# Second expert layer of an FFT-and-two-experts kernel: the last column block takes the seven-product form, block ends and quarter sums move

## The chip, the core and the metric

The kernel runs on one core of a Trainium2 chip. Its time is the device time of one execution in microseconds. The version before has a median of 963.82 us over 3 runs (963.35 to 965.81).

## The reference, cut to what matters

```python
def _attn_ref(x):                                  # x: (2, 3008, 256)
    X = np.fft.fft(x, axis=1)
    X = np.fft.fft(X, axis=2)
    return X.real
...
h = x @ w_in                                       # layer 1: (6016, 256) @ (256, 2048)
g = np.maximum(h, 0.0) + alpha * np.minimum(h, 0.0)
y = g @ w_out                                      # (2048, 256)
...
h = x @ w_in                                       # layer 2, same sizes, own weights
g = h * (1.0 / (1.0 + np.exp(-h)))
return (g @ w_out).astype(np.float32)
```

All values are fp32. The kernel splits each operand of a product into a rounded high part and a low rest, and forms a product as three matmuls: high by high, low by high, high by low.

## The kernel before

**Blocks and steps.** The 6016 tokens are handled, by a symmetry of the transform, as 6 column blocks c = 0 to 5 of 512 columns (448 in block 0 of layer 2), each for a sum and a difference half. Layer 1 takes 16 steps per block, 96 in all. Layer 2 takes 8 pairs p per block, 7 steps each; its steps are numbered on from 96 (block 0 is steps 96 to 151, block 1 begins at 152). Work beside the matmuls is tied to step numbers by tables (`T0`, `T1`, `PRE`, `WHEN`, `SUMS`), inside a manual schedule: every engine runs its instructions in the order in which the code issues them.

**Layer 2, one pair.** A 2x2 block product with seven instead of eight half-size products gives h: `trio` issues the seven as M1 to M7, three matmuls each (L875). VectorE and ScalarE add them to the four quarters c11, c12, c21, c22 (`ring`), and ScalarE applies SiLU. Then follows the product with `w_out2`. In blocks 0 and 5 this is `second2`: all eight quarter products, 24 matmuls a pair (L959); each quarter is split by a ScalarE copy (the high part, L894) and a VectorE or GpSimd subtraction (the low part, L899). In blocks 1 to 4 (`FAST`) the output product has the seven-product form as well: four differences T1 to T4 of the quarters (L1072), seven splits (h.. on ScalarE L1073, l.. on VectorE or GpSimd L1085), and seven groups O1 to O7 of three matmuls, 21 a pair (`group`, L1060), accumulated over the eight pairs in PSUM (O2 goes through a bank of its own and is added up by VectorE as E).

**Order in a fast pair.** `SEQ`, `SEQ0`, `SEQ1` and `SEQ2` are token lists, one token for one instruction or one group of three matmuls; "h21-1" is the high part of quarter 21 of the pair before. So the output product of a pair runs among the products of the next one. `SEQ1` (p = 1) also holds the end of the block before: two copies out of PSUM on ScalarE (m5c, m7c), and the adds U2, U3, U4, D12, D21 on VectorE and D22 on GpSimd (`ending`, L1110, L1129).

**Quarter sums and factors.** Each block's layer-1 result x2 is written out and also turned into four quarter sums in place, four GpSimd subtractions of 128x512 (`x2_sums`, L778), which begin three steps after the block's result is saved. Blocks 2 to 5 read these back in layer 2 (`load_raw32`) and split them, one factor a pair, by ScalarE (fh) and GpSimd (fl, L1019). Block 0's and 1's seven factors are made from x2 directly (`factors`, L827, L828, L832).

**Weights of layer 2.** They arrive as 64-bit integers' halves. `narrow` makes floats of them: two ScalarE instructions, a VectorE shift (L241) and an integer add (L243, on GpSimd in the first 16 steps, else on VectorE). Most converted weights are set aside in DRAM (`keep_back`, at the steps `PRE`) and fetched again later; `mixed_wout` and `store_s` (L285 to L298) form sums of the output weights on GpSimd. In layer 1 GpSimd also makes the low part of every activation (gl, L727).

Of the kernel before, what the change touches and what calls it, by code (L numbers as in the profile page):

```python
# [1532 lines left out]
```

## Time and profile before

| | before |
|---|---|
| median of 3 runs | 963.82 us |
| profiled execution, its own time | 967.2 us |
| span in the profile, first to last instruction | 965.3 us |
| mean granted TensorE clock | 0.991 |
| TensorE matmul busy | 939.8 us (97%) |
| VectorE busy | 754.3 us (78%) |
| ScalarE busy | 670.7 us (69%) |
| GpSimd busy | 534.9 us (55%) |

In the profile PE is TensorE, DVE is VectorE, ACT is ScalarE, POOL is GpSimd and SP the engine that issues most transfers. Matmuls overlap in it, so the busy time of PE counts more than what it could not do without; the distance between the starts of matmuls is the better measure.

### The profile page before, as it was taken

To read this page: it belongs to the slowest core of one execution; us is meant where nothing else is said; L and a number is where in the kernel's file an instruction comes from. 1 tells how busy PE (TensorE), PEld (TensorE's weight loads), DVE (VectorE), ACT (ScalarE), POOL (GpSimd) and SP (SyncE) were. 2 spreads that over 40 slices of the span, in tenths; PEclk is the share of its full clock that TensorE was granted. 3 is DMA by queue.
4 is the path that set the end of the run, shared out by engine and by line. 5 is a ranking of instruction groups with operands and counts; after the bars stand their busy time and mean duration, and the time that the engine had idled before them with its cause. 6 is when DMAs were issued, how large, how long until landed. Compare 5 with 4: busy or idle time off the path is not lost.

```text
span 965.3 us, 12665 instructions
## 1 busy us (share of the span) xinstructions
PE 939.8 (97%) x4261; PEld 773.2 (80%) x4261; DVE 754.3 (78%) x1113; ACT 670.7 (69%) x1168; POOL 534.9 (55%) x371
## 2 busy tenths in 40 slices
PE   9999999999999979999989999999999999998998
PEld 9899888888788868888879778768777777776886
DVE  4877665777787797866655689999999999988554
ACT  6887566665665656766655688878878888884554
POOL 0598777677688689999985522323332233232322
PEclk9999999999999999999999999999999999998999
DMA  9311123234616321012221034533344344440001
GB/s 342 138 44 50 50 58 75 55 94 135 216 57 238 109 102 66 29 39 77 66 87 34 31 119 152 173 119 125 134 158 145 117 142 142 154 142 33 12 1 43
DMA packets 50268, 98.99 MB, mean 103 GB/s; under 512 B 6326, under 2 KB 13596, under 8 KB 49180
## 3 DMA queue, kind: packets, MB, share of 16 engines
q1 hardware_dynamic: 49628, 97.36, 30.7%
q8 instruction: 33, 0.54, 0.2%
q10 hardware_dynamic: 576, 0.84, 0.2%
q14 instruction: 31, 0.25, 0.1%
HBM read 64.74 MB, written 33.44 MB: 102 GB/s over the span
## 4 chain that ended last, share of the span: by engine, by line
PE 84%; DVE 8%; issue 4%; ACT 1%; POOL 1%; DMA 1%; DVEq 0%; POOLq 0%; ACTq 0%
PE pso L742 25%; PE psh L875 19%; PE psh L651 13%; PE psm L1060 11%; PE pso L959 7%; PE psB L466 2%; DVE ring L1072 2%; PE psE L1060 2%; PE psU L1283 2%; PE psW L602 1%; DVE ghl L1085 1%; DVE ring L1071 1%; DVE ring L908 1%; DMA ur<-tmid 1%; DVE forms L1085 1%
## 5 line engine op out<-in xcount | busy, mean ns | idle before, releaser
L727 POOL TENSOR_TENSOR gl<-r,gh 128x1024 fp32r<-128x1024 f32 (+1 forms) x96 | 228.0, 2377 | 62.9 <-ACT gh L726 44.7
L875 PE MATMUL psh<-ts,wi 128*128 128x512 f32 (+1 forms) x864 | 238.1, 393 | 5.6 <-DVE ring L1071 3.0
L875 PEld LDWEIGHTS psh<-ts,wi 128*128 128x128 f32 x864 | 160.5, 189 | 48.0 <-DVE ring L1071 10.5
L742 PE MATMUL pso<-gh,wo_o 128*128 128x512 f32 (+1 forms) x768 | 192.8, 388 | 0.0
L742 PEld LDWEIGHTS pso<-gh,wo_o 128*128 128x128 f32 x768 | 145.1, 189 | 27.9
L651 PE MATMUL psh<-pq,wa 128*128 128x512 f32 (+1 forms) x576 | 149.5, 393 | 7.0 <-DVE h L671 7.0
L700 DVE SCALAR_TENSOR_TENSOR psd<-h,psh 128x512 f32<-128x512 f32 (+1 forms) x96 | 65.7, 684 | 98.9 <-PE psh L651 98.5
L651 PEld LDWEIGHTS psh<-pq,wa 128*128 128x128 f32 x576 | 107.5, 189 | 29.4 <-DVE h L671 8.9
L726 ACT ACTIVATE gh<-r 128x1024 fp32r<-128x1024 f32 (+1 forms) x96 | 99.9, 1041 | 36.2 <-DVE r L711 36.0
L1085 DVE TENSOR_TENSOR ghl<-ring,ghl 128x512 fp32r<-128x512 f32 x160 | 117.0, 754 | 0.4
L908 DVE TENSOR_TENSOR ring<-ring,psh 128x448 f32<-128x448 f32 (+1 forms) x112 | 71.3, 652 | 55.5 <-PE psh L875 53.4
L701 ACT ACTIVATE r<-psh 128x512 f32<-128x512 f32 (+1 forms) x96 | 56.6, 589 | 81.6 <-DVE psd L700 74.4
L1073 ACT ACTIVATE ghl<-ring 128x512 fp32r<-128x512 f32 x160 | 96.1, 625 | 10.9 <-DVE ring L1072 10.2
L742 PE MATMUL pso<-gl,wo_o 128*128 128x512 f32 (+1 forms) x384 | 101.4, 385 | 0.0
L1072 DVE TENSOR_TENSOR ring<-ring 128x512 f32<-128x512 f32 x128 | 92.5, 722 | 8.6 <-POOL forms L1085 3.5
L1019 POOL TENSOR_TENSOR ts<-sides,ts 128x512 fp32r<-128x512 f32 x21 | 34.7, 1651 | 109.1 <-ACT ts L1014 109.1
L959 PE MATMUL pso<-ghl,wAo 128*128 128x448 f32 (+1 forms) x324 | 86.1, 381 | 3.5 <-POOL ghl L899 3.5
L742 PEld LDWEIGHTS pso<-gl,wo_o 128*128 128x128 f32 x384 | 72.2, 188 | 13.5
L1085 POOL TENSOR_TENSOR forms<-ring,forms 128x512 fp32r<-128x512 f32 x32 | 41.7, 1302 | 72.5 <-ACT forms L1073 72.5
L1060 PE MATMUL psm<-ghl,sring 128*128 128x512 f32 x288 | 81.3, 396 | 0.0
L911 ACT ACTIVATE ring<-ring 128x448 f32<-128x448 f32 (+1 forms) x64 | 38.6, 602 | 59.8 <-DVE ring L908 59.2
L1073 ACT ACTIVATE ring<-psh 128x512 f32<-128x512 f32 x96 | 56.9, 592 | 33.4 <-PE psh L875 33.4
(145 smaller groups left out, 1616.7 us busy)
## 6 DMA issues: line engine op xcount, KB each, us to landing
sring<-sdr SPq DMA_DIRECT2D x32, 512.0 KB, 4.0
raw<-in_w_in SPq DMA_DIRECT2D x16, 512.0 KB, 5.6
raw<-in_w_out SPq DMA_DIRECT2D x16, 512.0 KB, 5.7
xf<-x SPq DMA_DIRECT2D x8, 1024.0 KB, 4.9
sides<-xf SPq DMA_DIRECT2D x28, 256.0 KB, 4.4
ts<-fdr SPq DMA_DIRECT2D x26, 256.0 KB, 3.6
fdr<-ts SPq DMA_DIRECT2D x24, 256.0 KB, 4.5
out_dram<-ob SPq DMA_DIRECT2D x19, 256.0 KB, 2.7
```

What stands on the lines that cost most here:

```text
L651: T.matmul(bank[:, :w], wa[q][:, mm, eo, a, :], pq[c][:, 2 * eo + bb, :w], start=eo == 0 and a == bb, stop=bb == 1, skip_group_check=True)
L700: V.scalar_tensor_tensor(other[:, :w], t[:, :w], 2.0, bank[:, :w], op0=ALU.mult, op1=ALU.subtract)
L726: A.activation(hi[:, :, :w], r[:, :, :w], AF.Copy)
L727: G.tensor_tensor(lo[:, :, :w], r[:, :, :w], f32(hi[:, :, :w]), op=ALU.subtract)
L742: T.matmul(po[c][s][k][:, :w], wo1[q][:, mm, a, k * P:(k + 1) * P], g[:, s, :w], start=m == 0 and a == 0 and g is hi, stop=m == NF - 1 and ...
L875: T.matmul(dst[:, :w], wi2[p][:, FORMS[j], a], t[:, :w], start=start and a == 0 and t is hi, stop=t is lo, skip_group_check=True)
L908: V.tensor_tensor(dst[:, :w], a[:, :w], bank[j][:, :w], op=ALU.add)
L959: T.matmul(po[c, 2][s][k][:, :w], wo2[q][:, mm + m, a, k * P:(k + 1) * P], outs[p, i][:, g, :w], start=p == 0 and i < 2 and a == 0 and g == 0,
L1060: T.matmul(dst, w, form[f][:, g], start=first and b == g == 0, stop=last and g == 1, skip_group_check=True)
L1072: sub = lambda dst, a, b: V.tensor_tensor(dst, a, b, op=ALU.subtract)
L1073: copy = lambda dst, src: A.activation(dst, src, AF.Copy)
L1085: (G if name in ON_G else V).tensor_tensor(form[f][:, 1], side_of[f], f32(form[f][:, 0]), op=ALU.subtract)
```

## The change

- `FAST` becomes 1 to 5: the last block takes the seven-product output form. Its last pair gets token lists of its own (`K5`, `L5`), and a list `Z` ends the kernel in place of `second2`'s last matmuls and `store`.
- Tokens are given per pair of a block (A, B, C, D, F, N, N, L for blocks 2 to 5; F0, F1, F2, N.. for block 1). A letter g at a token puts it on GpSimd; without it a low part or an add is VectorE's. A token that an earlier list already performed is skipped, so lists can run ahead.
- Block end: five accumulators are copied out by ScalarE (m1c, m3c, m4c, m5c, m7c); only U2 and E add out of PSUM on VectorE; five adds between SBUF tiles (a1 to a5) lie in the third to fifth pair of the next block on GpSimd (in `Z` on VectorE).
- Quarter sums: block 2's at steps 69, 72, 75, 78; block 3's at 103 to 108; block 5's at 126 to 139; block 4's result is read back from DRAM at step 111 (`again`) and summed at 115 to 124.
- `PRE` and `T1` get other steps, and one entry of `STAGE_B` is a step earlier. Block 0's end is stored by single tokens of F0.

```diff
-    FAST = 1, 2, 3, 4
+    FAST = 1, 2, 3, 4, 5
...
+    def again(c, steps):
+        t = spot("px2", [2, 2, CK * N2], F32, "x2")
+        nc.sync.dma_start(flat2(t), flat2(xf[c][0]))
+        SUMS[c] = steps
+        return x2_sums(c, t)
...
-        for _ in range(SUMS):
-            yield EARLY
-        for dst, a, b in ((b11, b12, b11), (b12, b22, b12), (b22, b22, b11), (b21, b21, b22)):
+        for i, (dst, a, b) in zip(SUMS[c], ((b11, b12, b11), (b12, b22, b12), (b22, b22, b11), (b21, b21, b22))):
+            while now[0] < i:
+                yield EARLY
             yield AMID
             SUB.tensor_tensor(dst, a, b, op=ALU.subtract)
...
+    def ending(c, name, other):
+
+        o, u, rest4 = outbuf(c), tail["u"], t1
+        add = lambda dst, a, b: (G if other else V).tensor_tensor(dst, a, b, op=ALU.add)
+        copies = {"m1c": (u, "O1"), "m3c": (o[:, 1, 0], "O3"), "m4c": (rest4, "O4"), "m5c": (o[:, 1, 1], "O5"),
+                  "m7c": (o[:, 0, 1], "O7")}
+        if name in copies:
+            dst, src = copies[name]
+            A.activation(dst, accum[c, src], AF.Copy)
+            copied.add((c, src))
         elif name == "U2":
-            add(u, u, accum[c, "O6"])
-        elif name == "U4":
-            add(o[:, 1, 0], u, o[:, 1, 1])
-        elif name == "D12":
-            add(o[:, 1, 0], o[:, 1, 0], accum[c, "O3"])
+            V.tensor_tensor(u, u, accum[c, "O6"], op=ALU.add)
+        elif name == "a1":
+            add(o[:, 1, 0], o[:, 1, 0], u)
+        elif name == "a2":
+            add(o[:, 1, 0], o[:, 1, 0], o[:, 1, 1])
             write(c, 1, 0)
...
-    ON_G = ('l11', 'fl', 'D22')
...
+        "N": ("h22-1 c12-1 l11-1g M1 E-2 s12-1 h21-1 m1 l22-1 T1-1 T3-1 hT1-1 fh M2 c11 O1-1 M6 u2 s11 O3-1 "
+              "lT1-1 hT3-1 O5-1 T2-1 hT2-1 M7 u3 l21-1 M5 lT3-1 T4-1 O7-1 lT2-1 c22 hT4-1 M4 fl O6-1 h11 "
+              "s21 s22 M3 lT4-1 O2-1 O4-1 "),
...
+        "L5": ("M1 m1 hT1-1 T3-1 l21-1 M2 c11 M6 O1-1 hT3-1 u2 T2-1 M7 T4-1 s11 lT1-1 h11 u3 M5 M4 l11 c22 "
+               "M3 hT2-1 lT3-1 hT4-1 lT2-1 s21 s22 O2-1 c12 O3-1 h21 O1 O6-1 O5-1 O7-1 lT4-1g s12 h22 E-1 "
+               "m1c l21 T1 hT1 l22 T3 O4-1 hT3 O2 T2 T4 O3 lT1 hT2 hT4 lT2 O6 lT3 "),
+        "Z": ("E-1 O7-1 O5-1 U2-1 m3c-1 m7c-1 lT4-1g a1-1 O4-1 m5c-1 a3-1 a2-1 m4c-1 a4-1 a5-1 "),
...
-    SUMS = 3
-    T1 = 42, 44, 48, 49, 50, 51, 52, 54, 54, 56, 58
+    SUMS = {2: (69, 72, 75, 78), 3: (103, 105, 106, 108), 5: (126, 132, 134, 139)}
+    AGAIN = 111, 4, (115, 118, 120, 124)
+    T1 = 40, 42, 46, 47, 48, 49, 50, 51, 53, 54, 55
```

Line numbers in the rows of the changed kernel are its own: 883 is `trio`, 1071 `group`, 1083 and 1084 the adds and subtractions of a pair, 1125 the copies of a block end, 1128 U2, 1120 the adds a1 to a5, 785 the quarter sums, 904 a low part in block 0.

On TensorE, at the end of the program (last pair of block 5; psh are products of `trio`, pso the output banks), 27 matmuls of `second2` stand behind the last product before, of which these are the last 19:

```order
L959 MATMUL pso_7782<-forms,wAo_4799 128x512
L959 MATMUL pso_7780<-ghl,wAo_4799 128x512 x2
L959 MATMUL pso_7782<-ghl,wAo_4799 128x512 x2
L959 MATMUL pso_7780<-ghl,wAo_4799 128x512
L959 MATMUL pso_7782<-ghl,wAo_4799 128x512
L959 MATMUL pso_7783<-forms,wAo_4799 128x512 x2
L959 MATMUL pso_7781<-forms,wAo_4799 128x512 x2
L959 MATMUL pso_7783<-forms,wAo_4799 128x512
L959 MATMUL pso_7781<-forms,wAo_4799 128x512
L959 MATMUL pso_7783<-ghl,wAo_4799 128x512 x3
L959 MATMUL pso_7781<-ghl,wAo_4799 128x512 x3
```

and now, from the last product on (psm and psE are the banks of `group`):

```order
L883 MATMUL psh_8256<-ts,wi_7_4661 128x512 x3
L1071 MATMUL psE<-ghl,wAo_4797 128x512 x3
L1071 MATMUL psm<-forms,sring 128x512 x3
L1071 MATMUL psm<-forms,wAo_4797 128x512 x3
L1071 MATMUL psm<-ghl,sring 128x512 x9
L1071 MATMUL psm<-ghl,wAo_4797 128x512 x6
L1071 MATMUL psm<-forms,sring 128x512 x3
L1071 MATMUL psm<-ghl,sring 128x512 x9
L1071 MATMUL psm<-ghl,wAo_4797 128x512 x3
```

The 27 have become 39: six groups of the pair before and the seven of the last pair itself.

On VectorE, in the second pair of block 3 (the end of block 2 lies there; ob is the output buffer, sides holds u and the running sum E), there stands before:

```order
L1071 TENSOR_TENSOR ring<-ring,psh_6387 128x512
L1071 TENSOR_TENSOR ob<-sides,psm 128x512
L1110 TENSOR_TENSOR sides<-sides,psm 128x512
L1110 TENSOR_TENSOR ob<-ob,sides 128x512
L1072 TENSOR_TENSOR ring<-ring 128x512
L1110 TENSOR_TENSOR ob<-sides,ob 128x512
L1085 TENSOR_TENSOR ghl<-ring,ghl 128x512
L1110 TENSOR_TENSOR ob<-ob,psm 128x512
L1071 TENSOR_TENSOR ring<-ring,psh_6466 128x512
L1072 TENSOR_TENSOR ring<-ring 128x512
L1085 TENSOR_TENSOR forms<-ring,forms 128x512
```

and now:

```order
L1083 TENSOR_TENSOR ring<-ring,psh_6474 128x512
L1128 TENSOR_TENSOR sides<-sides,psm 128x512
L1084 TENSOR_TENSOR ghl<-ring,ghl 128x512 x2
L1084 TENSOR_TENSOR ring<-ring 128x512
L1083 TENSOR_TENSOR ring<-ring,psh_6474 128x512
L1084 TENSOR_TENSOR ghl<-ring,ghl 128x512 x2
L1083 TENSOR_TENSOR ring<-ring,psh_6474 128x512
L1084 TENSOR_TENSOR forms<-ring,forms 128x512
```

Of the adds of the block end (four of the five before are shown, U2, U3, U4 and D12) U2 (L1128) is left; in the place of the others stand instructions of the pair itself.

On GpSimd, in layer 1 around step 70 (gl is the low part of an activation, x the layer-1 result of block 3 before and of block 2 now, stage_s sums of output weights, wi a layer-2 weight tile, pq one row of block 5's input), there stands before:

```order
L727 TENSOR_TENSOR gl<-r,gh 128x1024
L557 TENSOR_TENSOR pq_3120<-pb,pq_3120 1x512
L727 TENSOR_TENSOR gl<-r,gh 128x1024
L778 TENSOR_TENSOR x_3251<-x_3251 128x512
L298 TENSOR_TENSOR stage_s<-stage_s 128x4x128 x2
L727 TENSOR_TENSOR gl<-r,gh 128x1024
L778 TENSOR_TENSOR x_3251<-x_3251 128x512
L727 TENSOR_TENSOR gl<-r,gh 128x1024
L370 TENSOR_TENSOR wi_0_3262<-y_3341,wi_0_3262 128x4x128
```

and now, up to the same weight tile:

```order
L727 TENSOR_TENSOR gl<-r,gh 128x1024 x2
L298 TENSOR_TENSOR stage_s<-stage_s 128x4x128
L727 TENSOR_TENSOR gl<-r,gh 128x1024
L557 TENSOR_TENSOR pq_3113<-pb,pq_3113 1x512
L727 TENSOR_TENSOR gl<-r,gh 128x1024
L785 TENSOR_TENSOR x_2582<-x_2582 128x512
L727 TENSOR_TENSOR gl<-r,gh 128x1024
L370 TENSOR_TENSOR wi_0_3261<-y_3305,wi_0_3261 128x4x128
```

The two sums at this place are one, and the two L298 are further ahead, with a gl between them.

On GpSimd, in block 0 (steps 104 to 112: ghl a low part, wAo an output weight's low part), there stands before:

```order
L382 TENSOR_TENSOR wi_5_4425<-t_98,wi_5_4425 128x4x128
L778 TENSOR_TENSOR x_4448<-x_4448 128x512 x2
L899 TENSOR_TENSOR ghl<-ring,ghl 128x448
L778 TENSOR_TENSOR x_4448<-x_4448 128x512 x2
L324 TENSOR_TENSOR wAo_4176<-y_4506,wAo_4176 128x2x256
L324 TENSOR_TENSOR wAo_4538<-y_4508,wAo_4538 128x2x256
L899 TENSOR_TENSOR ghl<-ring,ghl 128x448
```

and now:

```order
L785 TENSOR_TENSOR x_3249<-x_3249 128x512
L382 TENSOR_TENSOR wi_5_4415<-t_98,wi_5_4415 128x4x128
L785 TENSOR_TENSOR x_3249<-x_3249 128x512 x2
L904 TENSOR_TENSOR ghl<-ring,ghl 128x448
L785 TENSOR_TENSOR x_3249<-x_3249 128x512
L324 TENSOR_TENSOR wAo_4166<-y_4498,wAo_4166 128x2x256
L324 TENSOR_TENSOR wAo_4528<-y_4500,wAo_4528 128x2x256
L904 TENSOR_TENSOR ghl<-ring,ghl 128x448
```

It is block 3's sums that stand here now, four as before, three of them ahead of the first low part.

## Rows read from the trace of the kernel before

**Rows 1.** The page: span, and TensorE's busy time and share of it.

```profile
span 965.3 us, 12665 instructions
PE 939.8 (97%) x4261; PEld 773.2 (80%) x4261; DVE 754.3 (78%) x1113; ACT 670.7 (69%) x1168; POOL 534.9 (55%) x371
```

**Rows 2.** Windows: block 0, 1, 2; block 5's first seven pairs; last pair.

```profile
core 0: us, PE busy (x) PEld busy (x) DVE busy (x) ACT busy (x) POOL busy (x), PEclk, DMA share, GB/s
463.30:543.20 79.90, 76.39 (x361) 68.77 (x360) 49.37 (x74) 48.90 (x90) 60.59 (x57) 0.98 0.18 58
543.20:625.30 82.10, 79.82 (x342) 62.37 (x341) 73.00 (x108) 66.47 (x121) 24.60 (x18) 1.00 0.39 129
625.30:705.70 80.40, 79.64 (x338) 61.73 (x337) 77.60 (x118) 67.42 (x123) 23.66 (x17) 1.00 0.43 141
...
866.70:945.80 79.10, 74.94 (x312) 60.71 (x313) 50.85 (x77) 42.22 (x71) 20.87 (x15) 0.96 0.04 14
945.80:965.30 19.50, 15.83 (x70) 12.76 (x68) 9.04 (x14) 8.21 (x14) 4.70 (x3) 1.00 0.14 54
```

**Rows 3.** Timeline of the end: start us, us, engine, instructions, [idle before <-releaser].

```profile
958.75 1.52 PE L959 MATMUL pso<-forms,wAo 128*128 128x512 f32 x6
...
960.11 1.52 PE L959 MATMUL pso<-ghl,wAo 128*128 128x512 f32 x6
...
961.67 0.60 ACT L972 ACTIVATE ob<-pso 128x512 f32<-128x512 f32 x1 [2.35 <-PE pso L959]
962.29 0.35 ACTq L976 DMA_DIRECT2D out_dram<-ob  x1
```

**Rows 4.** Timelines of VectorE and GpSimd in a steady pair of block 3.

```profile
764.26 1.19 DVE L1085 TENSOR_TENSOR ghl<-ring,ghl 128x512 fp32r<-128x512 f32 x1
...
767.65 2.13 DVE L1072 TENSOR_TENSOR ring<-ring 128x512 f32<-128x512 f32 x3
769.70 0.68 DVE L1085 TENSOR_TENSOR ghl<-ring,ghl 128x512 fp32r<-128x512 f32 x1
770.30 0.68 DVE L1071 TENSOR_TENSOR ring<-ring,psh 128x512 f32<-128x512 f32 x1
...
763.11 1.80 POOL L1019 TENSOR_TENSOR ts<-sides,ts 128x512 fp32r<-128x512 f32 x1 [5.69 <-ACT ts L1014]
765.88 1.30 POOL L1085 TENSOR_TENSOR forms<-ring,forms 128x512 fp32r<-128x512 f32 x1 [0.97 <-ACT forms L1073]
772.86 1.80 POOL L1019 TENSOR_TENSOR spare<-sides,spare 128x512 fp32r<-128x512 f32 x1 [5.68 <-ACT spare L1014]
```

**Rows 5.** Timeline of layer 1 around step 70.

```profile
349.30 8.67 DVE L243 CUSTOM_DVE_ANT_0 y<-raw,y 128x1024 uint16<-128x1024 uint16 x1
...
350.14 1.27 POOL L778 TENSOR_TENSOR x<-x 128x512 f32<-128x512 f32 x1
...
351.38 2.52 POOL L298 TENSOR_TENSOR stage_s<-stage_s 128x512 fp32r<-128x512 f32 x2
...
356.17 1.25 POOL L778 TENSOR_TENSOR x<-x 128x512 f32<-128x512 f32 x1
...
359.28 2.93 PE L651 MATMUL psh<-pq,wa 128*128 128x512 f32 x6 [5.52 <-DVE h L671]
```

**Rows 6.** Windows: three stretches in which the granted clock was 0.50.

```profile
358.10:364.80 6.70, 5.52 (x13) 4.36 (x14) 6.04 (x10) 5.09 (x9) 2.87 (x2) 0.50 0.29 81
491.20:494.50 3.30, 3.30 (x11) 2.91 (x10) 1.47 (x3) 1.66 (x4) 3.22 (x6) 0.50 0.00 0
873.50:876.80 3.30, 3.30 (x10) 2.53 (x9) 3.19 (x5) 1.36 (x3) 1.28 (x1) 0.50 0.03 5
```

**Rows 7.** Timeline of block 0 around step 115.

```profile
482.89 2.92 POOL L778 TENSOR_TENSOR x<-x 128x512 f32<-128x512 f32 x2
...
485.78 2.87 POOL L324 TENSOR_TENSOR wAo<-y,wAo 128x512 fp32r<-128x512 f32 x2
...
488.61 1.13 POOL L899 TENSOR_TENSOR ghl<-ring,ghl 128x448 fp32r<-128x448 f32 x1
489.79 0.47 PE L959 MATMUL pso<-ghl,wAo 128*128 128x448 f32 x1 [3.51 <-POOL ghl L899]
```

**Rows 8.** TensorE's timeline in block 5's first pairs, one wait.

```profile
871.03 0.96 PE L875 MATMUL psh<-ts,wi 128*128 128x512 f32 x3 [1.27 <-DVE ring L908]
```

More of the change, by code (lines that the diff above doesn't have):

```diff
@@ L1408 @@
         for n, (c, p) in enumerate(pairs):
-            slow = c not in FAST
-            text = {0: SEQ0, 1: SEQ1, 2: SEQ2}.get(p, SEQ)
-            if c in FAST:
-                if n == NF // 2:
-                    run(open_fast())
-                load_s(p)
+            if c not in FAST:
+                for j in range(7):
+                    ahead(step)
+                    if step == NC * NF:
+                        close1(last)
+                    product2(c, p, j)
+                    pull(CHUNKS[n][j])
+                    save_due()
+                    if n and j < 3:
+                        item(*pairs[n - 1], 7 + j)
+                    advance(MID1)
+                    item(c, p, j)
+                    advance(MID2)
+                    advance(MID3)
+                    advance(LATE)
+                    step += 1
+                queue.append(second2(c, p))
+                continue
+            if n == NF // 2:
+                run(open_fast())
+            load_s(p)
+            if c < NC - 1:
                 if p == 0:
@@ L1465 @@
-            for name, lag in rest_of:
-                perform(n - lag, name)
-            queue.append(second2(c, p))
-        for j in range(3):
-            item(*pairs[-1], 7 + j)
-        pull(24)
-        flush(0)
+            for name, lag, other in tokens(sequence(c, p)):
+                if name in CHAIN:
+                    ahead(step)
+                    j, side, start = CHAIN[name]
+                    if start and name != "M5":
+                        pair[n, side] = ptile([P, 512], "psh2", HALF[(n + side) % 2])
+                    trio(c, p, j, pair[n, side], start)
+                    if p == NF // 2 - 1 and c < NC - 1:
+                        refill(c, TURN.index(j))
+                    behind()
+                    step += 1
+                elif name[0] == "Q":
+                    pull(3)
+                elif name[0] in "io":
+                    last_items(*pairs[n - 1], name)
+                else:
+                    perform(n - lag, name, other)
@@ L1474, in _tokens @@
+        for name, lag, other in tokens("Z"):
+            perform(len(pairs) - lag, name, other)
 def _tokens():
```

195 lines of the change are left out of this document (70 added, 125 removed), and 28 rows, old and new, of the table SEQ.

## Prediction, on record before the changed kernel was run

> **What bounds the kernel now.** The page comes first: TensorE is busy for 97% of a span of 965.3 us [rows 1]. That share hides waits, because matmuls overlap. The last twelve matmuls start six per 1.36 us [rows 3], so one of 512 columns needs 0.227 us, and the reader should set each stage of the windows [rows 2] against its matmul count times that price. A fast pair has 42 matmuls, 9.52 us, a fast block eight, 76.2 us. Block 2 takes 80.4 us with VectorE busy for 77.6 of them: VectorE sets its pace, by 4.2 us (blocks 3 and 4 repeat it). Block 1 takes 82.1. Block 5's first seven pairs have 312 matmuls, 70.7 us, and take 79.1; there VectorE is busy for 50.9 us only, so these are single waits, such as the one for an add at 871 us [rows 8], and the half clock behind them. Its last pair and the end take 19.5.
>
> The timelines show two more stalls. At 349.3 us VectorE's integer add for a weight takes 8.67 us, while GpSimd runs one instruction behind the other until 357.4; TensorE waits 5.5 us at 359.3 [rows 5], and then runs 6.8 us at the granted clock 0.50 [rows 6], the lower of its two levels (1.2 of 2.4 GHz), which it had after this idle time: half of that is lost too. Together 9.1 us. At 489.8 TensorE waits 3.5 us for a low part that stands on GpSimd behind four quarter sums and two weight parts [rows 7], and runs 3.4 us at 0.50 afterwards: 5.2 us.
>
> **The change, part by part.** All terms are counted on the span.
>
> *Layer 1 (quarter sums, PRE).* Where the add met 350.1 to 357.4 without a gap, there stood two quarter sums (1.27 and 1.25 us), two L298 (2.52) and two gl [rows 5]. Now one sum stands there, and the L298 are ahead, a gl between them. In all, layer 1 keeps four of twelve sums, some 10 us less on GpSimd. Gain between 9.1 (the whole stall) and nothing (another of the adds meets a run as long: GpSimd is still used nearly through behind step 70). I take 7.1, nearer to the whole, since the run that made it is taken apart. The Trainium skill bears on this place ("SBUF — State Buffer", section "SBUF: two separate sides"): a VectorE instruction with two SBUF inputs and a GpSimd instruction exclude each other, and whichever starts first holds the shared ports for its whole length. By that alone the add would have come in at 350.1, behind one instruction, and a new collision could take back at most one gl's length, so that this term would be near 9. The trace disagrees: the add waited through six instructions and ended when GpSimd had nothing more to do. I go by the row.
>
> *Block 0.* Four sums still stand ahead of the low part that was late, block 3's instead of block 5's, but three of the four come ahead of an earlier low part, and none waits for the store of a result. It is ready about 2 us earlier, so the wait falls from 3.5 to some 1.6. Against this, block 4's four sums (5.1 us at 1.27) now follow, the first behind a 1 MB load that itself waits for a store, at a place where GpSimd has few gaps; TensorE, no longer held up, comes earlier for the next low parts. Bounds: gain 5.2, loss 2 (the added 5.1 less the 3 to 4 us that a low part has in hand). I take a gain of 1.5. Block 5's sums, at 126 to 139, fall on GpSimd's idle time in the second half (60.6 of 79.9 us busy [rows 2]). The earlier factors of block 1 free VectorE and GpSimd for its first pairs.
>
> *Block 1.* 82.1 us now. The matmul floor is 21 products, 24 old outputs of 448 columns (0.2 us each) and seven pairs of 9.52: 76.2. With what the plain pairs keep (below) 79.1: gain 3.0, between 1 and 4.5.
>
> *Blocks 2 to 4.* VectorE loses four adds of the block end and one low part (lT1, lT2) in two pairs, and gets three fl and five l11 back: 119 instructions instead of 117 (counted in the order of the program). GpSimd has 14 instead of 16. So the sum must come from the price of an instruction. Independent ones start 0.60 us apart (769.70, 770.30), three that build on each other 0.7 [rows 4]; fl on GpSimd (1.80) keeps a VectorE low part waiting, 1.19 instead of 0.68, while l11 (1.30) lies beside instructions that read PSUM and costs little. Three fl on VectorE cost 0.60 each instead of 0.5 of waiting: no loss. A plain pair N has 15 VectorE instructions, 15 x 0.60 + 0.1 = 9.1 us, under the 9.52 of TensorE; today's takes 9.75 (fl at 763.11 and 772.86). The first five pairs have 74: 44.4, some 1.2 for dependences, 11 GpSimd instructions at about 0.25: 48.4. They take 80.4 - 3 x 9.75 = 51.2 now. With 9.65 for N the block comes to 77.4; since the terms leave no slack I take 78.4: 2.0 a block, 6.0 in all. Bounds: TensorE's floor (4.2 a block) and today's rate, 77.6 / 117 x 119 plus today's 2.8 us of idle time: a loss of 1.3 a block. The copies m3c and m4c add 1.2 us to ScalarE (0.60 each [rows 3]), which is busy for 67.4 of 80.4 us; a1 to a5 lie on GpSimd, idle for 56 of 80.4 us. Nothing waits for them but the stores.
>
> *Block 5, first seven pairs.* Three matmuls fewer in each pair. Seven eighths of 78.4 are 68.6; K5 has 17 VectorE instructions, 1.2 more: 69.8 instead of 79.1, a gain of 9.3. Bounds: 12.4 (floor 66.7) and 7.6 (104 instructions at today's rate and 2.5 idle, 71.5).
>
> *The end.* Here the last pair's own output product can't lie beside later products. Now: 19.5 us, of which 3.1 pass behind the end of the last ScalarE copy (962.27 [rows 3]). After: TensorE has 63 matmuls, 14.3 us, but VectorE 28 instructions one after the other: 16.8, six that need the one ahead 0.7, the third group of c12 behind c22 0.5, the GpSimd low part lT4 against VectorE's 0.5, the backlog of K5 0.9, half clock in TensorE's gaps 0.5, and the same 3.1: 23.0. A loss of 3.5, between 1 and 6.
>
> Sum: -7.1 - 1.5 - 3.0 - 6.0 - 9.3 + 3.5 = -23.4 us. The profiled execution took 967.2 us, 3.4 more than the median of the timed runs; from that median 963.8 - 23.4 = 940.4 us.
>
> **Rivals.** *VectorE keeps today's rate.* Speaks for it: 77.6 of 80.4 us busy, and two instructions more. Then blocks 2 to 4 lose 4, block 1 gains 1, block 5's pairs gain 7.6, the end loses 5, layer 1 and block 0 as above: 963.8 - 8.2 = 955.6. Against it: the low part of 1.19 us, half a microsecond a pair that goes with fl.
>
> *GpSimd's queue only moves its pile.* Another integer add meets a gapless run in layer 1 (nothing gained there), and block 4's sums hold up block 0 (loss 2): 963.8 - 12.8 = 951.0. For it: the added 5.1 us and the load; against it: the four removed per block of layer 1.
>
> *Slower: the ports decide.* The 65 GpSimd instructions of the fast blocks have two SBUF inputs. If each holds VectorE for its whole 1.30 us, a block has 71.4 + 1.4 + 14 x 1.3 = 91 us, 10.6 more than now; three blocks +32, block 1 +3, block 5 -3, the other terms -8.6: 987. The rule of the page named above has this outcome, wherever a VectorE low part stands beside a GpSimd instruction; 764.26 [rows 4] shows it at half a microsecond. It decides from 0.7 us of wait a pair on (23.4 + 2.9 over 40 pairs). Against it: the other GpSimd instruction of the pair costs VectorE no more than 0.2 today.
>
> *No change:* the end loses what the pairs gain (loss over 12): the three other terms would have to fail as well.
>
> **Numbers.** Forecast 0.62, today's rate 0.13, GpSimd's pile 0.17, ports 0.05, no change 0.03. A measurement of this kernel tells about 0.3% (2.9 us) from nothing. All but the last two are faster: faster 0.92, same 0.03, slower 0.05. The range goes to the two faster rivals, to 955; downwards to 930, where most terms reach their floors (floors alone: 963.8 - 9.1 - 5.2 - 4.5 - 12.6 - 12.4 + 1 = 921). The forecast's own range is 935 to 947.
>
> **What would show it.** No integer add over 3 us and no clock of 0.50 around step 70; a wait under 2 us around step 112; blocks 2 to 4 at 77 to 79.5 us with VectorE under 97%; block 5's seven pairs at 68 to 71.5; 21 to 25.5 from its last pair on. Wrong if a fast block takes 80 us or more, if a weight's add is caught again, or if TensorE waits in the second half of a pair for an lT4 or l11 by more than half a microsecond.

## The result, and the profile after

The changed kernel takes 977.49 us (median of 4 runs, 975.08 to 978.16) beside 964.82 us of the kernel before in the same comparison: ratio 1.012, 95% interval 1.0083 to 1.0157. It is 1.2% slower; the forecast was 940.4, 2.4% faster than before. The profiled execution took 975.08 us with a span of 973.3, 8.0 more than before [rows 1].

The page of the changed kernel has TensorE less and VectorE more busy than before, by 5.6 and 47.3 us:

```profile
span 973.3 us, 12677 instructions
PE 934.2 (96%) x4237; PEld 764.2 (79%) x4237; DVE 801.6 (82%) x1163; ACT 692.0 (71%) x1219; POOL 524.3 (54%) x357
```

Windows of the changed kernel, cut where a stage's first product starts: layer 1, blocks 0 to 4 of layer 2, block 5's first seven pairs, and the rest (columns as in [rows 2]):

```profile
40.00:457.70 417.70, 413.65 (x1915) 345.69 (x1914) 309.16 (x442) 275.74 (x452) 335.85 (x216) 1.00 0.26 81
457.70:540.90 83.20, 77.44 (x362) 68.19 (x360) 50.49 (x73) 47.24 (x89) 70.02 (x63) 0.98 0.27 94
540.90:622.90 82.00, 79.70 (x340) 62.79 (x341) 75.72 (x112) 67.77 (x125) 22.63 (x15) 1.00 0.39 129
622.90:707.60 84.70, 80.22 (x338) 62.12 (x337) 83.93 (x120) 68.00 (x126) 22.94 (x14) 1.00 0.42 134
707.60:792.30 84.70, 80.24 (x337) 62.13 (x336) 83.85 (x120) 67.94 (x125) 22.94 (x14) 1.00 0.41 133
792.30:877.00 84.70, 80.22 (x337) 62.12 (x336) 83.89 (x120) 67.97 (x125) 22.94 (x14) 1.00 0.42 134
877.00:949.00 72.00, 68.49 (x295) 54.74 (x295) 69.69 (x102) 57.95 (x105) 16.60 (x11) 1.00 0.21 66
949.00:973.30 24.30, 16.47 (x64) 11.02 (x62) 20.47 (x30) 13.04 (x24) 2.90 (x2) 0.96 0.18 65
```

Beside [rows 2] (of blocks 3 and 4, which are not printed there, block 3 took 80.4 us before and block 4 80.6) this gives the prediction's sum term by term:

| stage | predicted | measured |
|---|---|---|
| layer 1 | -7.1 | -5.6 |
| block 0 | -1.5 | +3.3 |
| block 1 | -3.0 | -0.1 |
| blocks 2, 3, 4 | -2.0 each | +4.3, +4.3, +4.1 (12.7) |
| block 5, first seven pairs | -9.3 | -7.1 |
| end | +3.5 | +4.8 |
| sum | -23.4 | +8.0, as the spans |

Most of the loss is in blocks 2 to 4. VectorE had 118 instructions in 77.60 us before [rows 2] and has 120 in 83.9 now: two more instructions, six microseconds more. Some of them have become longer. VectorE's and then GpSimd's timeline in the second pair of block 3 (columns as in [rows 3]):

```profile
721.10 0.68 DVE L1128 TENSOR_TENSOR sides<-sides,psm 128x512 f32<-128x512 f32 x1
721.70 2.39 DVE L1084 TENSOR_TENSOR ghl<-ring,ghl 128x512 fp32r<-128x512 f32 x2
724.12 1.67 DVE L1084 TENSOR_TENSOR ring<-ring 128x512 f32<-128x512 f32 x1
725.71 0.68 DVE L1083 TENSOR_TENSOR ring<-ring,psh 128x512 f32<-128x512 f32 x1
726.31 2.88 DVE L1084 TENSOR_TENSOR ghl<-ring,ghl 128x512 fp32r<-128x512 f32 x2
...
720.32 1.44 POOL L1084 TENSOR_TENSOR ghl<-ring,ghl 128x512 fp32r<-128x512 f32 x1 [6.14 <-ACT ghl L1085]
721.72 1.82 POOL L1030 TENSOR_TENSOR ts<-sides,ts 128x512 fp32r<-128x512 f32 x1
723.50 3.43 POOL L1120 TENSOR_TENSOR ob<-ob,sides 128x512 f32<-128x512 f32 x2
726.89 1.75 POOL L1120 TENSOR_TENSOR ob<-ob 128x512 f32<-128x512 f32 x1
```

L1128 and L1083 read a PSUM bank and take 0.68 us here as anywhere. L1084 reads two SBUF tiles and takes 1.67 us (724.12), or some 1.8 for one of the two in a group of 2.39, while GpSimd runs without a gap from 720.32 to 728.64. GpSimd's adds a1, a3 and a2 (L1120) take 1.72 to 1.75 us there, where a GpSimd instruction of the same size took 1.30 [rows 4]. The lists place these adds at the end of the third and the start of the fourth pair. A list orders instructions within an engine; GpSimd had nothing ahead of them to wait for, and ran them more than a pair early. In the same way a4 and a5 ran in the third pair instead of the fifth.

Added up over block 3, VectorE's instructions with two SBUF inputs that take more than 0.75 us exceed the usual 0.69 by 10.2 us in the changed kernel, and by 3.7 us in the kernel before. This sum is called VectorE's wait below. Its rise, 6.5 us, is about as large as the six microseconds.

### The profile page after: what moved, and what is told of

It is laid out like the page before. It is cut to its first block, busy times and chain, and to the rows that moved or that the text cites. A ratio compares the mean times of both kernels' runs of the same rounds, so it can differ in the third digit from the quotient of the medians.

```text
span 973.3 us, 12677 instructions
## 1 busy us (share of the span) xinstructions
PE 934.2 (96%) x4237; PEld 764.2 (79%) x4237; DVE 801.6 (82%) x1163; ACT 692.0 (71%) x1219; POOL 524.3 (54%) x357
## 4 chain that ended last, share of the span: by engine, by line
PE 62%; DVE 22%; issue 5%; POOL 4%; ACT 4%; DMA 3%; SPq 0%; DVEq 0%; ACTq 0%; POOLq 0%
PE pso L742 25%; PE psh L651 13%; PE psh L883 10%; DVE ghl L1084 8%; PE psm L1071 7%; DVE ring L1084 5%; DVE ring L1083 4%; DVE forms L1084 2%; PE psB L466 1%; PE psE L1071 1%; PE psW L602 1%; POOL x L785 1%; PE psU L1315 1%; POOL ghl L904 1%; DMA x<-in_x 1%
## 5 line engine op out<-in xcount | busy, mean ns | idle before, releaser
L1084 DVE TENSOR_TENSOR ghl<-ring,ghl 128x512 fp32r<-128x512 f32 x186 | 148.0, 824 | 0.6 <-ACT ghl L1085 0.3
L1085 ACT ACTIVATE ghl<-ring 128x512 fp32r<-128x512 f32 x200 | 122.2, 625 | 34.0 <-DVE ring L1084 32.7
L1084 DVE TENSOR_TENSOR ring<-ring 128x512 f32<-128x512 f32 x160 | 125.3, 783 | 2.5
L1084 POOL TENSOR_TENSOR forms<-ring,forms 128x512 fp32r<-128x512 f32 x19 | 32.3, 1702 | 167.8 <-ACT forms L1085 167.8
L1071 PE MATMUL psm<-ghl,sring 128*128 128x512 f32 x360 | 99.9, 393 | 6.8 <-DVE ghl L1084 6.7
L1085 ACT ACTIVATE ring<-psh 128x512 f32<-128x512 f32 x120 | 71.2, 593 | 24.5 <-PE psh L883 22.6
L1091 ACT ACTIVATE ring<-ring 128x512 f32<-128x512 f32 x120 | 74.4, 626 | 19.7 <-DVE ring L1083 19.2
L1071 PEld LDWEIGHTS psm<-ghl,sring 128*128 128x128 f32 x360 | 66.9, 188 | 25.9 <-DVE ghl L1084 11.5
L1083 DVE TENSOR_TENSOR ring<-ring,psh 128x512 f32<-128x512 f32 x120 | 81.6, 680 | 5.8 <-PE psh L883 3.5
L711 DVE SCALAR_TENSOR_TENSOR r<-r,al,psh 128x512 f32<-128x512 f32 (+1 forms) x96 | 70.7, 736 | 10.3 <-ACT r L701 9.0
```

Of the source, the lines that this page charges most:

```text
L711: V.scalar_tensor_tensor(r[:, s, :w], r[:, s, :w], al[:, m:m + 1], h[:, :w], op0=ALU.mult, op1=ALU.add)
L1071: T.matmul(dst, w, form[f][:, g], start=first and b == g == 0, stop=last and g == 1, skip_group_check=True)
L1084: sub = lambda dst, a, b: eng.tensor_tensor(dst, a, b, op=ALU.subtract)
L1091: A.activation(side_of[f], x if f == "21" else side_of[f], AF.Silu)
```

## The experiments

Ratios are against runs of the kernel before in the same comparison. Two tables serve several experiments. The first has spans, and stages measured from first product to first product:

| kernel | span | ratio, 95% interval | layer 2 begins | block 0 | block 3 |
|---|---|---|---|---|---|
| e1, tables only | 963.5 | 0.9997 (0.998 to 1.0015) | 457.94 | 83.4 | 80.5 |
| e2, reload later | 967.8 | 1.0022 (1.0007 to 1.0037) | 458.29 | 77.2 | 84.6 |
| e3, adds on VectorE | 967.9 | 1.0054 (1.0038 to 1.0069) | 456.20 | 84.0 | 84.2 |
| e4, last block only | 960.5 | 0.9939 (0.9914 to 0.9964) | 458.72 | 84.3 | 80.5 |
| e5, e4 and reload later | 952.5 | 0.9868 (0.9853 to 0.9882) | 458.04 | 77.1 | 80.4 |
| e6, one memset per add | 957.3 | 0.9921 (0.9906 to 0.9936) | 458.06 | 83.4 | 80.2 |
| e7, adds spread | 974.0 | 1.0078 (1.0059 to 1.0098) | 459.52 | 83.4 | 84.2 |
| e8, e5 with fl and end on VectorE | 955.7 | 0.9889 (0.9864 to 0.9915) | 459.09 | 76.9 | 81.5 |
| e9, best stages joined | 952.1 | 0.9853 (0.9833 to 0.9872) | 459.15 | 76.9 | 80.4 |
| e10, one copy per add | 961.9 | 0.9952 (0.9935 to 0.9969) | 458.42 | 84.0 | 81.4 |
| e11, e9 and D22 on VectorE | 953.5 | 0.9861 (0.9844 to 0.9878) | 460.87 | 78.5 | 80.0 |
| e12, three memsets per add | 957.3 | 0.9934 (0.9906 to 0.9961) | 458.14 | 83.7 | 80.2 |

The second has the eight pairs of block 3, each from the start of its first product to that of the next pair:

| block 3, pair | 0 | 1 | 2 | 3 | 4 | 5 | 6 | 7 |
|---|---|---|---|---|---|---|---|---|
| before | 10.71 | 11.09 | 9.95 | 9.52 | 9.88 | 9.77 | 9.73 | 9.75 |
| changed | 10.67 | 11.60 | 12.91 | 10.47 | 9.52 | 10.05 | 9.69 | 9.84 |
| e7, spread | 10.70 | 11.01 | 10.98 | 11.57 | 9.52 | 10.28 | 10.28 | 9.84 |
| e10, copies | 10.65 | 10.36 | 10.84 | 10.48 | 9.52 | 10.04 | 9.67 | 9.85 |
| e12, three memsets | 10.66 | 10.09 | 9.89 | 10.49 | 9.52 | 10.04 | 9.69 | 9.84 |
| e12, block 5 (no factors; K5 in pair 6) | 10.66 | 9.52 | 9.54 | 9.52 | 9.52 | 9.52 | 10.46 | |

**e1: the tables of quarter sums, PRE, T1 and STAGE_B in the kernel before.**

```diff
-    SUMS = 3
+    SUMS = {2: (69, 72, 75, 78), 3: (103, 105, 106, 108), 5: (126, 132, 134, 139)}
+    AGAIN = 111, 4, (115, 118, 120, 124)
```

> The kernel before with the new steps of the quarter sums (the reload of block 4's result included), of PRE, T1 and STAGE_B, and nothing else. If layer 1 and block 0 move by these tables alone, layer 1 gains 5 to 6 us (it ends at 457 to 458 us), block 0 takes about 83 us instead of 79.9, all later stages stay as before (80.4 a fast block), and the whole is 2 to 3 us faster than before. If the loss in block 0 comes from the new block 1 (its lists and the earlier end of block 0), block 0 stays near 80 and the whole is 5 to 6 us faster.

Measured: no difference in the timed runs, where 2 to 3 us less were expected; the profiled execution is 1.8 us shorter. In it layer 1 is 5.4 us shorter than in the trace of before, block 0 is 3.5 and block 1 1.3 us longer (83.4 both, beside [rows 2]), and block 5's first seven pairs are 1.5 us shorter. So block 0's loss comes with the tables, not with the new block 1.

**e2: the changed kernel, block 4's reload and sums later.**

```diff
-    AGAIN = 111, 4, (115, 118, 120, 124)
+    AGAIN = 119, 4, (124, 126, 128, 130)
-    SUMS = {2: (69, 72, 75, 78), 3: (103, 105, 106, 108), 5: (126, 132, 134, 139)}
+    SUMS = {2: (69, 72, 75, 78), 3: (103, 105, 106, 108), 5: (132, 134, 137, 140)}
```

> The changed kernel with the reload of block 4's result at step 119 instead of 111, so behind the two weight loads that stood behind it, its sums at 124, 126, 128, 130 and block 5's at 132, 134, 137, 140. If the reload, which waits for a store, kept the weight load back in the queue and so GpSimd idle for 5 us, that idle time goes, and block 0 falls from 83.2 to 78 to 80 us: 3 to 5 us faster than the changed kernel. If it is the number of sums on GpSimd (eight more than before), block 0 stays above 82.

Block 0 falls from 83.2 to 77.2 us, somewhat under the 78 to 80 expected, and the fast blocks stay: the loss in block 0 goes with the early reload and the sums that were moved along with it. The traces show what the reload held up. Timelines of the changed kernel, of GpSimd and of SP's queue:

```profile
481.02 1.51 POOL L904 TENSOR_TENSOR ghl<-ring,ghl 128x448 fp32r<-128x448 f32 x1
487.49 0.46 POOL L373 TENSOR_TENSOR t<-y 128x128 f32<-128x128 f32 x1 [4.95 <-DMA y<-stash_i]
...
478.20 0.32 SPq L789 DMA_DIRECT2D xf<-x  x1
482.07 0.32 SPq L774 DMA_DIRECT2D x<-xf  x1
482.49 0.85 SPq L311 DMA_DIRECT2D y<-stash_i  x2
```

The reload (L774) goes into the buffer that block 3's store (L789) reads, so it waits 3.5 us for that store. The weight's loads (L311) stand behind it in SP's queue and start at 482.49, and GpSimd, which needs them, idles for 4.95 us with the low parts (L904) queued behind. The same of e2:

```profile
483.88 0.47 POOL L373 TENSOR_TENSOR t<-y 128x128 f32<-128x128 f32 x1 [0.77 <-DMA y<-stash_i]
...
478.78 0.32 SPq L789 DMA_DIRECT2D xf<-x  x1
480.04 1.95 SPq L311 DMA_DIRECT2D y<-stash_i  x2
482.96 0.32 SPq L774 DMA_DIRECT2D x<-xf  x1
```

Here the loads go first. TensorE's waits for GpSimd's low parts in block 0 of the changed kernel (us in total, times, longest):

```profile
PE pso L977 <- POOL ghl L904: 5.6, 5, 1.9
```

and in e2:

```profile
PE pso L977 <- POOL ghl L904: 1.9, 1, 1.9
```

**e3: the changed kernel, a1 to a5 on VectorE** (the letter g dropped at these five tokens).

```diff
-              "h21 fl-1g a1-3g l22 O4-1 "),
-        "D": ("M1 m1 a3-4g M2 a2-4g hT3-1 O1-1 fh M6 c11 T2-1 hT1-1 O3-1 u2 lT3-1 M5 s11 lT1-1 M7 O5-1 "
+              "h21 fl-1g a1-3 l22 O4-1 "),
+        "D": ("M1 m1 a3-4 M2 a2-4 hT3-1 O1-1 fh M6 c11 T2-1 hT1-1 O3-1 u2 lT3-1 M5 s11 lT1-1 M7 O5-1 "
...
```

> The changed kernel with the five adds a1 to a5 of each block end on VectorE instead of GpSimd: 124 VectorE instructions a block instead of 119, 9 on GpSimd instead of 14. If the blocks are slow because GpSimd instructions hold VectorE's two-input ones at 1.1 us each, five times 0.6 us come and about five times 1.1 go: blocks 2 to 4 at 81.5 to 83.5 us instead of 84.7, the kernel 4 to 10 us faster than the changed one. If they are slow because VectorE has more to do, each takes 3 us more, 87.7, and the kernel is 9 us slower.

Blocks 2 to 4 take 82.9, 84.2 (over the expected 83.5) and 83.0: five instructions more on the engine that sets the pace, and 0.5 to 1.8 us less time. VectorE has 82.04 us for 125 instructions instead of 83.93 for 120:

```profile
622.16:705.06 82.90, 79.18 (x337) 62.19 (x336) 82.04 (x125) 67.93 (x126) 14.47 (x9) 1.00 0.42 137
```

VectorE's wait in block 3 falls from 10.2 to 5.6 us. So it isn't VectorE's count that lost the time, and work given to GpSimd cost VectorE more than doing it itself.

**e4: the lists of before in blocks 2 to 4 and from block 1's fourth pair on, the rest of the change left in.**

```diff
-            return "ABCDFNNL"[p] if c > 1 else "NNNNNNNL"[p]
+            if c == NC - 1 and p > 2:
+                return "P" if p == 3 else "N"
+            return {0: "S0", 1: "S1", 2: "S2"}.get(p, "S") if c > 1 else "S"
```

S, S0, S1, S2 are the former lists with the former block end; P is N for the pair in which one gives way to the other.

> The changed kernel with the old token lists and the old block ends in blocks 1 to 4 (block 1's first three pairs stay new); the last block with the seven-product output, old lists in its first three pairs, N in three, then K5, L5 and Z. If the loss lies in the new lists, blocks 2 to 4 go back to 80.4 us, block 5's first seven pairs take 70.5 to 72 and the end 24 to 25: 12 to 14 us faster than the changed kernel, 2 to 5 faster than before. If it lies elsewhere (memory, the last block's preparation, the moved sums), blocks 2 to 4 stay above 83.

The span is 960.5 us, 12.8 less than the changed kernel's, as expected, and the timed runs are 0.6% faster than before: the last block's new form gains, the new lists of blocks 2 to 4 lose.

**e5: e4 with e2's two lines.**

> The kernel with the old lists in blocks 1 to 4 and the last block in the new form, and in addition block 4's reload at step 119 with its sums at 124 to 130 and block 5's sums at 132 to 140. Theory (the reload in front of a weight's load in SP's queue cost block 0 some 6 us): block 0 falls from 84.3 to 77.2, all else stays, span 953.4, about 955.3 us, 1.2 to 1.4% faster than before. Rival (the later sums are late for block 1's and block 2's factors, or block 1 gets the pile): block 1 or 2 gives 2 us or more of it back, 957.5.

The span is 952.5 us: block 0 falls by 7.2, and nothing is given back. Together the two repairs make a slower change a faster one, by 1.3%.

**e6, e10 and e12: what in an add on GpSimd costs.** The changed kernel with another instruction in the place of a1 to a5, in the same queue and the same place; the sums of the block ends are left out. The three added lines are those of e6, e10 and e12.

```diff
-        add = lambda dst, a, b: (G if other else V).tensor_tensor(dst, a, b, op=ALU.add)
+        add = lambda dst, a, b: G.memset(dst, 0.0) if other else V.tensor_tensor(dst, a, b, op=ALU.add)
...
+        add = lambda dst, a, b: G.tensor_copy(dst, b) if other else V.tensor_tensor(dst, a, b, op=ALU.add)
...
+        add = lambda dst, a, b: [G.memset(dst, 0.0) for _ in range(3)] if other else V.tensor_tensor(dst, a, b, op=ALU.add)
```

> The changed kernel, with each of the adds a1 to a5 on GpSimd (20 in all) replaced by a memset of the tile that it wrote; the sums of the block ends are left out by that. The instructions stand in the same place of the same queue, but read no SBUF. Theory (the adds read two SBUF tiles while VectorE does, and each holds up the other): blocks 2 to 4 take 80.2 to 81.5 us instead of 84.7, with the pairs 1 and 2 at 10.1 and 9.9 instead of 11.6 and 12.9; block 5's pairs 1 and 2 lose some 2.5; span 957 to 961. Rival (any GpSimd instruction there costs VectorE the same, or it is the lists' order that costs): 84.7 stays, span 973.

> The changed kernel with a1 to a5 on GpSimd as copies of their second operand to the same tile: one SBUF input instead of two (memsets: none). The sums of the block ends are left out by that. Theory (what VectorE's two-input instructions wait for is a GpSimd instruction that reads SBUF, as the Trainium skill's page SBUF — State Buffer, section SBUF: two separate sides, has it): pairs 1 and 2 of blocks 2 to 4 are slow again, 11.0 to 11.6 and 11 to 12.9, a block 82 to 84.7, more the longer a copy takes. Rival (only GpSimd instructions with two SBUF inputs hold VectorE up): 80.2 as with memsets.

> The changed kernel with each of a1 to a5 on GpSimd as three memsets of the tile that it wrote, so that GpSimd is busy for about as long as with an add (3 x 0.525 = 1.6 us; an add 1.6 to 1.74) and reads nothing. The sums of the block ends are left out by that. Theory (GpSimd's reading of SBUF is what VectorE's two-input instructions wait for): blocks 2 to 4 stay at 80.2 to 80.5 us as with one memset, span 957. Rival (only the time for which GpSimd is busy counts, so that one memset cost nothing because it is short): as long as the adds, 83.5 to 84.7 a block, span 968 to 973.

With memsets a block takes 80.2 us, one or three in the place of an add. With copies it takes 81.4, less than the 82 to 84.7 that were expected and more than the rival's 80.2. The same stretch as shown above, in e12, VectorE and then GpSimd:

```profile
717.95 2.38 DVE L1084 TENSOR_TENSOR ghl<-ring,ghl 128x512 fp32r<-128x512 f32 x2
720.37 0.69 DVE L1084 TENSOR_TENSOR ring<-ring 128x512 f32<-128x512 f32 x1
720.98 0.68 DVE L1083 TENSOR_TENSOR ring<-ring,psh 128x512 f32<-128x512 f32 x1
721.58 1.29 DVE L1084 TENSOR_TENSOR ghl<-ring,ghl 128x512 fp32r<-128x512 f32 x2
...
717.96 1.83 POOL L1030 TENSOR_TENSOR ts<-sides,ts 128x512 fp32r<-128x512 f32 x1
719.73 4.97 POOL L1120 MEMSET ob<- 128x512 f32 x9
```

Nine memsets run for 5 us beside VectorE's two-input instructions, and these take 0.69 us (720.37) and 1.29 for two (721.58): it is neither GpSimd's being busy nor its writing that they wait for. Beside the low part fl (L1030), which reads two SBUF tiles and stays as it was, the group of 717.95 takes 2.38 us here, as in the changed kernel (2.39). The copies read one tile and cost a block 1.2 us, 0.24 each; the adds read two and cost 4.5, 0.9 each. GpSimd's groups of L1120 in blocks 2 to 4 of the changed kernel (busy us, mean ns):

```profile
L1120 POOL TENSOR_TENSOR ob<-ob 128x512 f32<-128x512 f32 x6 | 10.4, 1740 | 0.0
L1120 POOL TENSOR_TENSOR ob<-ob,sides 128x512 f32<-128x512 f32 x6 | 10.3, 1728 | 0.0
L1120 POOL TENSOR_TENSOR ob<-ob,t 128x512 f32<-128x512 f32 x3 | 4.8, 1616 | 0.2
```

and in e10:

```profile
L1120 POOL COPY ob<-sides 128x512 f32<-128x512 f32 x6 | 6.3, 1076 | 0.0
L1120 POOL COPY ob<-ob 128x512 f32<-128x512 f32 x6 | 5.1, 843 | 0.0
L1120 POOL COPY ob<-t 128x512 f32<-128x512 f32 x3 | 2.9, 958 | 0.2
```

A copy is also shorter, so these runs don't tell whether the second input or the length makes an add dearer. The Trainium skill ("SBUF — State Buffer", section "SBUF: two separate sides") says that a VectorE instruction with two SBUF inputs and a GpSimd instruction that reads SBUF shut each other out; memsets at 80.2 and adds at 84.7 agree with it.

**e7: the five adds one by one**, each behind a GpSimd instruction that waits for its own pair.

```diff
-        "D": ("M1 m1 a3-4g M2 a2-4g hT3-1 O1-1 fh M6 c11 T2-1 hT1-1 O3-1 u2 lT3-1 M5 s11 lT1-1 M7 O5-1 "
+        "D": ("M1 m1 M2 hT3-1 O1-1 fh M6 c11 T2-1 hT1-1 O3-1 u2 lT3-1 M5 s11 lT1-1 M7 O5-1 "
...
+              "l21-1 T4-1 hT2-1 u3 hT4-1 h11 c22 lT2-1 O7-1 M4 lT4-1 M3 O6-1 s21 O2-1 c12 fl-1g a3-4g s12 l11 "
...
+        "N": ("h22-1 c12-1 l11-1g a4-6g a5-7g M1 E-2 s12-1 h21-1 m1 l22-1 T1-1 T3-1 hT1-1 fh M2 c11 O1-1 M6 u2 s11 O3-1 "
...
+              "lT3-1 l21-1 O5-1 hT2-1 lT2-1 T4-1 M7 s11 u3 O7-1 M5 M4 hT4-1 O6-1 c22 s21 fl-1g a2-5g h11 "
```

> The changed kernel, with a1 to a5 one each behind a GpSimd instruction that waits for its own pair (fl of pairs 1, 2 and 3, l11 of pairs 5 and 6), so that GpSimd can't run ahead with them. Theory one (each meeting of a GpSimd instruction with a two-SBUF-input instruction costs VectorE about 1 us, wherever it is): the cost only moves, from pairs 1 and 2 to all the pairs; a block takes 83 to 84.2 us, 0.5 to 1.7 less than 84.7, the slack of TensorE-bound pairs taking a part. Theory two (only the unbroken run of five to seven GpSimd instructions hurts): 80.2 to 81.5 a block. Theory three (instruction count on VectorE): 84.7.

84.2 a block: the unbroken run isn't the trouble. Set against e12, a1 costs 0.92 us in pair 1, a3 1.09 in pair 2, a2 1.08 in pair 3; a4 and a5 cost 0.24 and 0.59 in pairs 5 and 6, where VectorE has some room under TensorE's pace. Each add pays about a microsecond wherever VectorE sets the pace.

**e8: e5 with fl on VectorE in blocks 1 to 4, and no low part on GpSimd from K5 on.**

```diff
-        "S1": ("c12-1 s11-1 E-2 h11-1 U2-2 m7c-2 s12-1 l11-1g m5c-2 U3-2 T1-1 h21-1 M1 M2 m1 s22-1 U4-2 l21-1 M6 h22-1 fl-1g ...
+        "S1": ("c12-1 s11-1 E-2 h11-1 U2-2 m7c-2 s12-1 l11-1g m5c-2 U3-2 T1-1 h21-1 M1 M2 m1 s22-1 U4-2 l21-1 M6 h22-1 fl-1 ...
...
-        "Z": ("E-1 O7-1 O5-1 U2-1 m3c-1 m7c-1 lT4-1g a1-1 O4-1 m5c-1 a3-1 a2-1 m4c-1 a4-1 a5-1 "),
+        "Z": ("E-1 O7-1 O5-1 U2-1 m3c-1 m7c-1 lT4-1 a1-1 O4-1 m5c-1 a3-1 a2-1 m4c-1 a4-1 a5-1 "),
```

The same in S, S0, S2, and at l22-1, lT2-1, l22 of K5 and lT4-1 of L5.

> The kernel with old lists and late reload, and in two places that the stages tell apart: in blocks 1 to 4 the factor's low part fl is VectorE's instead of GpSimd's in every pair (one VectorE instruction more a pair, one GpSimd instruction less); and from K5 on no low part is GpSimd's. Theory (a meeting costs 1 us, an instruction 0.60): blocks 2 to 4 take 79 to 80 us instead of 80.4, the end 23.9 instead of 24.5. Rival (VectorE's count at its rate of 0.66): seven instructions more make a block 83 to 85 and the end, with one more, 25.

Half of it held. The end falls from 24.6 to 23.4 us and K5's pair from 10.46 to 9.69. But a block takes 81.5, 1.1 more than in e5. In e5 VectorE's wait in block 3 is 3.7 us, all beside the seven fl: 0.5 on average and not 1, less than the 0.60 of an instruction. The pairs that follow the plain list don't move: 9.52, 9.86, 9.74, 9.80, 9.73 instead of 9.52, 9.88, 9.74, 9.75, 9.75.

**e9 and e11: the best stages joined.** e9 is e5 with fl on VectorE in the second pair of a block (S1) and no low part on GpSimd from K5 on; in e11 the block end's D22 is VectorE's too.

```diff
-        "S1": ("... M1 M2 m1 s22-1 U4-2 l21-1 M6 h22-1 fl-1g D12-2 u2 c11 O1-1 T3-1 M7 l22-1 hT1-1 u3 lT1-1 T2-1 M5 D22-2g ...
+        "S1": ("... M1 M2 m1 s22-1 U4-2 l21-1 M6 h22-1 fl-1 D12-2 u2 c11 O1-1 T3-1 M7 l22-1 hT1-1 u3 lT1-1 T2-1 M5 D22-2 ...
```

> Old lists in blocks 1 to 4, new last block, late reload, no low part on GpSimd from the last pair but one on, and in the second pair of each block (where the block end's adds stand) the factor's low part on VectorE. From the stages of the two kernels that it joins: 952.5 less 0.8 in pair 6 of block 5, 1.2 in the end, and 0.65 in the second pair of blocks 2 to 4: span 948.6, 950.4 us, ratio 0.983. Rival (the three gains overlap, what a pair saves is waited for in the next): 951 to 952 span.

> The kernel of the best stages, and the block end's D22 on VectorE too, so that the second pair of a block has only l11 on GpSimd. One GpSimd instruction with two SBUF inputs less, some 1.0 us where VectorE has no slack, one VectorE instruction more, 0.6: each of blocks 2 to 5 gets 0.2 to 0.5 faster, 947 span. Rival (the add lies beside instructions that read PSUM, and costs nothing on GpSimd): 0.6 slower a block, 951.

e9's second pair stays at 11.09. In e8 it took 10.42, behind a first pair of 11.73 instead of 10.7: there fl had moved the time, not saved it. The end and K5's pair give 1.3 us, and layer 1, which has the same program, takes 1.1 more: 952.1 instead of the 948.6 expected, within 0.1 of the rival's 951 to 952. In e11 a block of 2 to 4 takes 80.0, 0.4 less, as D22's price says, but block 5's first seven pairs take 0.3 more; layer 1 and block 0 take 3.3 us more than e9's in that execution, and the span is 953.5, not 947. The timed runs of e5, e9 and e11 (954.19, 954.0, 954.87 us) can't be told apart: 1.3 to 1.5% faster than before, where the changed kernel is 1.2% slower.

## Why the prediction was wrong

**The step that failed: "11 GpSimd instructions at about 0.25".** The sum for blocks 2 to 4 gave VectorE a wait of 0.25 us for each GpSimd instruction, and called a1 to a5 free because GpSimd is idle for 56 us of a block; blocks 2 to 4 were to have VectorE under 97%, and have it at 99%. It asked whether GpSimd has time, not what VectorE pays. The price came from the 0.5 us at 764.26 and from an l11 that lay beside PSUM-reading work [rows 4]: the cheap ends of one cause. The 0.25 fits the old lists, where VectorE's wait is 3.7 us for 16 GpSimd instructions. In the new ones it is 10.2 us for 14, 0.73 each; in the first five pairs, for which the prediction put in 11 x 0.25 = 2.75, it is 8.5. Measured, the five adds cost 4.5 us a block (84.7 with them, 80.2 with e12's memsets).

The remaining 1.8 to the forecast 78.4 goes with what is left of VectorE's wait, 5.6 us in e12: by the trace 3.4 of them lie beside the four fl, and 2.2 beside two low parts, which in the old lists cost nothing. Block 5 of e12, which runs the same lists without fh and fl, takes 48.8 us for its first five pairs where block 3 takes 50.7. A run of the new lists without this work on GpSimd was not made, so this part is read from the traces and not tested.

The rival "the ports decide" had this mechanism and the side, at a chance of 0.05. Its price of 1.3 us for all 14 GpSimd instructions was too high (91 us a block, against 84.7), and its sum leaves out the end's 3.5 (some 990 instead of 987). The point that it named for the decision, 0.7 us of wait a pair, was passed: VectorE's wait rose by 0.8 us a pair (from 3.7 to 10.2 over eight pairs).

**Block 0** was to gain 1.5 and lost 3.3. The load that waits for a store was named and bounded by what the added sums need on GpSimd. What stands behind the load in SP's queue was left out: a weight's loads, and through them GpSimd's low parts. The one wait that the prediction counted, at 1.6 us, has become five of at most 1.9, together 5.6. With the reload behind them (e2) the stage gains 2.7, more than predicted.

**Block 1** gained 0.1 instead of 3.0. Its estimate was TensorE's floor, 76.2, and 2.9 for what the plain pairs keep, for which no working is given; at the prediction's own 9.65 a pair it would be 0.9 for seven. The plain pairs (3 to 7) take 49.3 us, 1.7 over their floor; the first three take 32.7 (11.36, 10.44, 10.94), 4.1 over theirs, and for these nothing of their own had been put in. In the third VectorE is busy for 10.87 of 10.94 us, with 2.6 us of wait beside GpSimd; what holds the first two stays open.

**Layer 1**: right in mechanism, 5.6 instead of 7.1. One of the two sums and the L298 are gone from the place, no integer add is over 2.2 us, and the clock stays at 1.00 there; but a shift is caught. VectorE, GpSimd and TensorE of the changed kernel:

```profile
353.43 4.82 DVE L241 TENSOR_SCALAR y<-y 128x512 int32<-128x512 int32 x1 [0.17 <-ACT y L235]
...
353.90 1.29 POOL L370 TENSOR_TENSOR wi<-y,wi 128x512 fp32r<-128x512 f32 x1
355.16 2.38 POOL L727 TENSOR_TENSOR gl<-r,gh 128x1024 fp32r<-128x1024 f32 x1
357.50 0.45 POOL L373 TENSOR_TENSOR t<-y 128x128 f32<-128x128 f32 x1
...
359.55 1.78 PE L651 MATMUL psh<-pq,wa 128*128 128x512 f32 x6 [1.68 <-DVE h L671]
```

The wait is 1.7 us instead of 5.5 [rows 5]. The profiled executions of the changed kernel and the twelve experiments, all with this layer 1, begin layer 2 between 456.2 and 460.9, so the term holds to some 2 us.

**Block 5's seven pairs** were right in mechanism: 72.0 instead of 69.8. Pairs 1 and 2 hold block 4's adds, 11.58 and 10.69 instead of 9.5 (e12), 3.2 us; where no adds and no factors stand, a pair takes TensorE's 9.52, less than the estimate's 9.65.

**The end** was right in mechanism, 24.3 instead of 23.0: VectorE has 30 instructions in that window instead of 28, and is busy for 20.47 us. The prediction put in 0.5 us for one low part on GpSimd; there are two, and beside each a low part on VectorE takes 1.1 us longer (1.78 and 1.77). Taking GpSimd's low parts away gains 0.5 to 1.3 there (24.6 in e5; 24.1, 23.4 and 23.3 in e9, e8 and e11).

## What to carry to other kernels

Before moving an elementwise instruction to an idle GpSimd, ask what it reads and what VectorE does meanwhile: beside VectorE work with two SBUF inputs an add of two SBUF tiles cost the busy engine 0.9 us here, more than the 0.6 of doing it there. The price goes with the place: by the traces a GpSimd fl cost VectorE 0.5 on average in the old lists and 0.85 in the new ones, so a price read off one order can't be carried to another. A place in a list isn't a time; GpSimd, with little to do, ran the adds more than a pair ahead of it. A transfer that waits for another held up the loads queued behind it (4.95 us of idle time on GpSimd), so put such a transfer behind the loads that someone waits for.
